# Attention and SwiGLU on one core: loads of batch 0 pair by pair, products from unit 5 on, and the rest tokens placed last in X

## The chip, the cores and the metric

The kernel runs on one core of one Trainium2 chip. The metric is the device time of one execution in microseconds (us), as a median of several. Before the change it is 454.04 us (three runs, 453.96 to 454.45). The profile is of one further execution, with a span of 453.1 us from the first to the last instruction.

## The reference, cut to what matters

Attention with 8 batches, 12 heads, 448 tokens and 64 values per head comes first; its output, as 3584 rows of 768, is the input of a SwiGLU block with 1536 inner columns.

```python
def _attn_ref(q, k, v):                      # (8, 12, 448, 64) each
    scale = 1.0 / np.sqrt(q.shape[-1])
    scores = scale * np.matmul(q, k.transpose(0, 1, 3, 2))
    scores = scores - np.max(scores, axis=-1, keepdims=True)
    attn = np.exp(scores)
    attn = attn / (np.sum(attn, axis=-1, keepdims=True) + 1e-09)
    return np.matmul(attn, v)

def _moe_ref(x, w_gate, w_val, w_out):       # x: (3584, 768)
    g = x @ w_gate                           # w_gate, w_val: (768, 1536)
    silu = g * (1.0 / (1.0 + np.exp(-g)))
    val = x @ w_val
    return silu * val @ w_out                # w_out: (1536, 768)
```

Inputs and output are float32. The kernel casts to fp16 while it loads.

## The kernel before

Two heads are one pair; there are 48 pairs, six per batch. The 448 keys of a pair are cut into four chunks of 112. The first 24 steps of the program are *units* (pair and chunk of batch 0); after them come *visits*, which mix chunks of later pairs with pieces of the SwiGLU block.

Loads of q, k, v and weights are requests of GpSimd (they cast). `load_qk16(pr, n)` fetches n pairs of q and k, `load_v(pr, n)` the values of n pairs, 112 KB a pair as fp16; `copy_v` moves the values beside a column of ones.

```python
        load_qk16(1, 1)
        make_identity(nc, ident)
        load_qk16(2, 1)
        load_qk16(3, 1)
        load_v(0, GP)              # GP = 3 pairs in one request
        load_qk16(4)               # two pairs
        load_v(3, GP)
        dummy(7)                   # filler matmuls
        prep(0)()
        dummy(1)
        turn = prep(1)
        wq = {                     # pair -> requests given out at its chunk 1
            0: [("qk", 6), ("g", 0), ("v", 0)],
            1: [("qk", 8), ("g", 1), ("v", 1)],
            3: [("qk", 10), ("V", 2), ("g", 2), ("v", 2)],
            4: [("g", 3), ("v", 3), ("qk", 12)],
            6: [("V", 3), ("o", 0)],
            7: [("o", 1)],
        }
```

In the program's list of waits each GpSimd request waits for the landing of the eighth request before it, as eight semaphores serve them in turn.

`prep(pr)` turns q and k of a pair, so that the 64 values lie on partitions: on TensorE for pairs 1 to 10, by DMA transposes (L168, L172) from pair 11 on. `qk` forms the scores of a chunk (L218) and takes their exponential on ScalarE (L226). `pv_chunk` multiplies it with values (L244, L252). The queries of a pair are cut into three blocks of 128 and a *rest* of 64, tokens 0 to 63; the two heads' rests share one block of 128 partitions. After the fourth chunk the sums are normalized into `xt`, and `turn_x` turns `xt` into X, the input of the SwiGLU block: channels on partitions, tokens along.

```python
        nc.vector.reciprocal(r[:, 0:7], a7[:, :, D])                      # L264
        nc.vector.tensor_tensor(xt..., a7[:, 0:n, 0:D], r..., ALU.mult)   # L265, n = 7 if pr < 12 else 6
        if pr < XPE:                                                      # XPE = 12
            return
        for hx in range(2):                                               # L274: the rest, pairs from 12 on
            nc.vector.tensor_scalar(xt[0:D, 3, ts(hx, D)], a7[ts(hx, D), 6, 0:D], r[ts(hx, D), 6:7], None, ALU.mult)
    # ... turn_x(pr) ...
        if pr < XPE:
            # tp is a PSUM tile
            for j in range(3):                                            # L292
                nc.tensor.matmul(tp[:, ds(D + 128 * j, 128)], lhsT=xt[:, j], rhs=ident[:], start=True, stop=True)
            for hx in range(2):                                           # L296: the rest
                nc.tensor.matmul(tp[ts(hx, D), 0:D], lhsT=xt[:, 3, 0:D], rhs=ident[:, ts(hx, D)], start=True, stop=True)
            nc.vector.tensor_copy(dst, tp[:, 0:S])                        # L303
            return
        nc.sync.dma_start_transpose(dst[:, D:S]..., xt[:, 0:3]...)        # L305
        nc.sync.dma_start_transpose(dst[:, 0:D]..., xt[0:D, 3])           # L308
```

The loop over units, with `dst` above being the pair's 448 tokens of X:

```python
        XAT = (11, 15, 17, 20)                       # units that begin with a turn_x
        for u in range(FIRST * NC):                  # 24 units
            pr, c = divmod(u, NC)
            qk(pr, c)
            # ... units 1 and 3: fillers and the turn of pair 1; unit 4: prep(2)()
            elif u >= 6 and c == 2:
                prep(pr + 2)()                       # pairs 3 to 7; pair 6 in unit 18
            if u in (5, 6, 7):
                dummy(1)
            if u in (6, 14):
                for p in range(3):
                    copy_v(u // 8 * 3 + p)
            if c == 1:
                for w in wq.pop(pr, []):
                    emit(w)
            if u in XAT:
                turn_x(XAT.index(u))
            for _ in range(1 if c == 2 or u in XAT else 2):
                if u >= 8 and pieces[0][0] * NC + pieces[0][1] <= u - 3:
                    piece()                          # one pv_chunk
```

The SwiGLU block works on blocks of 384 or 512 columns of X: block 0 on tokens 0 to 383 of batch 0, block 1 on the last 64 of batch 0 and all of batch 1, and so on. Each step makes a gate group `gp` and a value group `vp` of six matmuls (L317); the second part multiplies with `wo` (L362), evicts on ScalarE (L369) and writes rows of the output (L381).

Of the kernel before, what the change touches and what calls it, by code (L numbers as in the profile page):

```python
# [13 lines left out]
ALU = mybir.AluOpType  # L14
# [4 lines left out]
GP = 3  # L19
# [3 lines left out]
FIRST = 6  # L23
WIDE = 8
XPE = 12
# [8 lines left out]
def kernel(  # L34
# [14 lines left out]
    P = 112  # L49
# [6 lines left out]
    GPB = NHP // GP  # L56
    sm_scale = float(D) ** -0.5
    OH = DM // 2

    tabs = list(get_activation_tables(nc.m.arch).keys())  # L60

# [56 lines left out]
    def load_qk16(pr, n=2):  # L118
        h0 = 2 * (pr % 2) if pr >= 14 else 0
        if h0 == 0:  # L120
            q16 = raws.tile([P, 4, NC, D], FP16, tag="rq", bufs=RB, name="q16")
            k16 = raws.tile([P, 4, NC, D], FP16, tag="rk", bufs=RB, name="k16")
            pairbuf[:] = [q16, k16]
        q16, k16 = pairbuf
        for dst, src in ((q16, q), (k16, k)):
            flat = src.rearrange("b h s d -> (b h) s d")[2 * pr : 2 * pr + 2 * n]
            nc.gpsimd.dma_start(dst[:, ds(h0, 2 * n)], flat.rearrange("h (p c) d -> p h (c d)", c=NC))  # L127
        for i in range(n):
            h = h0 + 2 * i
            raw[pr + i] = (q16[:, h : h + 2], k16[:, h : h + 2])  # L130

    def load_v(pr, n=1):
        b, h = divmod(2 * pr, H)
        nc.gpsimd.dma_start(  # L134
            vraw[:, ds(pr % VS, n)].rearrange("p r h c d -> p (r h) (c d)"),
            v[b, h : h + 2 * n].rearrange("h (p c) d -> p h (c d)", c=NC),
        )

    def copy_v(pr):
        nc.vector.tensor_copy(Vts[pr % NV][:, :, :, 0:D], vraw[:, pr % VS])  # L140
# [91 lines left out]
                between()  # L232

    accs = {}

    def pv_chunk(pr, c):
        if c == 0:
            accs[pr] = ps_f.tile([128, 512], FP32, tag="f", name="acc")
        e = Es[pr % NE]
        vo = Vts[pr % NV]  # L240
        a7 = accs[pr][:, 0 : 7 * (D + 1)].rearrange("p (s d) -> p s d", s=7)
        for j in range(3):
            for hx in range(2):
                nc.tensor.matmul(  # L244
                    a7[:, 2 * j + hx],
                    lhsT=e[:, ds(c * EB + 9 * hx + 2 * j, 2)].rearrange("p b x -> p (b x)"),
                    rhs=vo[:, hx, c, 0 : D + 1],
                    start=c + j + hx == 0,
                    stop=False,
                )  # L250
        for hx in range(2):
            nc.tensor.matmul(  # L252
                a7[:, 6],
                lhsT=e[:, ds(c * EB + 6 + hx, 2)].rearrange("p b x -> p (b x)"),
                rhs=vo[:, hx, c, 0 : D + 1],
                start=False,
                stop=c == NC - 1 and hx == 1,
            )
        if c < NC - 1:
            return  # L260
        r = attp.tile([128, 8], FP32, tag="R", bufs=2, name="R")
        xt = Xts[pr % NX]
        n = 7 if pr < XPE else 6
        nc.vector.reciprocal(r[:, 0:7], a7[:, :, D])  # L264
        nc.vector.tensor_tensor(  # L265
            xt[:].rearrange("p j (h d) -> p (j h) d", h=2)[:, 0:n],
            a7[:, 0:n, 0:D],
            r[:, 0:n].unsqueeze(2).to_broadcast([128, n, D]),
            ALU.mult,
        )  # L270
        if pr < XPE:
            return
        for hx in range(2):
            nc.vector.tensor_scalar(  # L274
                xt[0:D, 3, ts(hx, D)], a7[ts(hx, D), 6, 0:D], r[ts(hx, D), 6:7], None, ALU.mult
            )

    def pv(pr):
        for c in range(NC):
# [2 lines left out]
    def turn_x(pr):  # L282
        b, hp = divmod(pr, NHP)
        kk, bb = divmod(b, NB)
        if kk not in X:
            X[kk] = xp.tile([128, NCB, NB * S], FP16, tag="X", name="X")
        dst = X[kk][:, hp, ts(bb, S)]
        xt = Xts[pr % NX]
        if pr < XPE:
            tp = accs[pr] if pr < FIRST else ps_f.tile([128, 512], FP32, tag="f", name="xtp")  # L290
            for j in range(3):
                nc.tensor.matmul(  # L292
                    tp[:, ds(D + 128 * j, 128)], lhsT=xt[:, j], rhs=ident[:], start=True, stop=True
                )
            for hx in range(2):
                nc.tensor.matmul(  # L296
                    tp[ts(hx, D), 0:D],
                    lhsT=xt[:, 3, 0:D],
                    rhs=ident[:, ts(hx, D)],
                    start=True,  # L300
                    stop=True,
                )
            nc.vector.tensor_copy(dst, tp[:, 0:S])  # L303
            return
        nc.sync.dma_start_transpose(  # L305
            dst[:, D:S].rearrange("p (j q) -> p j q", j=3), xt[:, 0:3].rearrange("p j m -> p (j m)")
        )
        nc.sync.dma_start_transpose(dst[:, 0:D].rearrange("p (j q) -> p j q", j=1), xt[0:D, 3])  # L308

    gate_small = [False]  # L310

# [32 lines left out]
    def ffn2_steps(kk, c0, n, hts, first, last_block):  # L344
        chunks = range(n // 128)
        if first:
            steps = [(ch, oh) for oh in range(2) for ch in chunks]
        else:
            steps = [(ch, oh) for ch in chunks for oh in range(2)]
        osbs = {}  # L350
        for ch, oh in steps:
            last = last_block and ch == n // 128 - 1
            if last or oh == 0:
                osbs[ch] = fp.tile([128, DM], FP32, tag="osb", bufs=3, name="osb")
            osb = osbs[ch]
            parts = [(oh * OH, OH)]
            if last and oh:
                parts = [(OH, OH // 2), (OH + OH // 2, OH // 2)]
            for m0, w in parts:
                op = ps_f.tile([128, 512], FP32, tag="f")  # L360
                for fb in range(NFB):
                    nc.tensor.matmul(  # L362
                        op[:, 0:w],
                        lhsT=hts[:, fb, ts(ch, 128)],
                        rhs=wo[oh][:, fb, ds(m0 - oh * OH, w)],
                        start=(fb == 0),
                        stop=(fb == NFB - 1),
                    )
                nc.scalar.activation(osb[:, ds(m0, w)], op[:, 0:w], AF.Copy, scale=1.0 / HS)  # L369
                if not last:  # L370
                    m0, w = 0, DM
                    if oh == 0:
                        continue
                l0 = c0 + ch * 128
                l = l0
                while l < l0 + 128:
                    b, j = divmod(l, S)
                    c, p0 = divmod(j, P)
                    m = min(P - p0, l0 + 128 - l)
                    eng = nc.scalar if last and m < 64 else nc.sync  # L380
                    eng.dma_start(  # L381
                        out[ts(NB * kk + b, S), :].rearrange("(p c) m -> c p m", c=NC)[
                            c, p0 : p0 + m, ds(m0, w)
                        ],
                        osb[l - l0 : l - l0 + m, ds(m0, w)],
                    )
                    l += m
            yield NFB * OH / 2400.0

# [6 lines left out]
    with tc.manual_schedule():  # L396
# [4 lines left out]
        for vo in Vts:  # L401
            nc.vector.memset(vo[:, :, :, D:], 1.0)
        load_qk16(1, 1)
        make_identity(nc, ident)
        load_qk16(2, 1)
        load_qk16(3, 1)
        load_v(0, GP)
        load_qk16(4)
        load_v(3, GP)
        dummy(7)  # L410
        prep(0)()
# [1 line left out]
        turn = prep(1)  # L413

        wq = {
            0: [("qk", 6), ("g", 0), ("v", 0)],
            1: [("qk", 8), ("g", 1), ("v", 1)],
            3: [("qk", 10), ("V", 2), ("g", 2), ("v", 2)],
            4: [("g", 3), ("v", 3), ("qk", 12)],
# [45 lines left out]
        def share(total, at, n):  # L465
            return (at + 1) * total // n - at * total // n

        XAT = (11, 15, 17, 20)
        pieces = [(p, c) for p in range(FIRST) for c in range(NC)]

        def piece():
# [2 lines left out]
        for u in range(FIRST * NC):  # L474
            pr, c = divmod(u, NC)
            qk(pr, c)
            if u == 1:
                dummy(1)
                turn()
                dummy(1)  # L480
            elif u == 3:
                dummy(2)
            elif u == 4:
                prep(2)()
            elif u >= 6 and c == 2:
                prep(pr + 2)()
            if u in (5, 6, 7):
                dummy(1)
            if u in (6, 14):
                for p in range(3):  # L490
                    copy_v(u // 8 * 3 + p)
            if c == 1:
                for w in wq.pop(pr, []):
                    emit(w)
            if u in XAT:
                turn_x(XAT.index(u))
            for _ in range(1 if c == 2 or u in XAT else 2):
                if u >= 8 and pieces[0][0] * NC + pieces[0][1] <= u - 3:
                    piece()

        queue = []
# [126 lines left out]
```

The softmax here doesn't subtract the row's maximum and nothing guards it: scores larger than these inputs give would overflow.

## Time and profile before

| engine or transfer | busy, us | share of 453.1 us |
|---|---|---|
| TensorE matmuls (PE) | 443.6 | 98% |
| TensorE weight loads (PEld, beside the matmuls) | 247.1 | 55% |
| VectorE (DVE) | 201.3 | 44% |
| ScalarE (ACT) | 239.1 | 53% |
| GpSimd (POOL) | 138.0 | 30% |
| GpSimd's DMA queue | 23.37 MB | 41.7% of 16 DMA engines |
| SyncE's DMA queue | 24.66 MB | 29.6% of 16 DMA engines |

"PE" counts a matmul from its start to its modelled end, and matmuls overlap, so its share says that the engine is occupied, not that it is at its peak. A wait is shown in brackets after an instruction: the time for which the engine stood idle before it, and what ended that. GpSimd's requests and SyncE's DMA instructions are shown with the time that it took to issue them; the landing is a number of its own ("DMA to landing").

### The profile page before, as it was taken

Reading aid. Unit: us, or ns where it says so; the run is one execution under the profiler, and the core shown is the slowest. Engines: PE = TensorE matmul, PEld = TensorE weight load, DVE = VectorE, ACT = ScalarE, POOL = GpSimd, SP = SyncE. Lnnn points to the kernel's source line nnn. Section 1 sums busy time; section 2 is a strip of 40 time slices with the busy share of each in tenths; the row PEclk is TensorE's granted clock in tenths of the full one; section 3 lists DMA queues with packets and bytes.
Section 4 is the critical chain, followed back from the end, with each engine's and each line's share of the span. In section 5 each row is a group of like instructions: output and inputs, shape, how many; then the busy total and the mean of one; then the engine's idle time right before and its main releaser. Section 6 shows DMA issues by size and latency. Waiting matters only on the chain.

```text
span 453.1 us, 9845 instructions
## 1 busy us (share of the span) xinstructions
PE 443.6 (98%) x4007; PEld 247.1 (55%) x4007; DVE 201.3 (44%) x456; ACT 239.1 (53%) x350; POOL 138.0 (30%) x222
## 2 busy tenths in 40 slices
PE   8889999999999999999999999999999999999996
PEld 3555655645455656545456665545455656644464
DVE  3555653356563535354443553444354444145400
ACT  6874576766555555645556446644654644222222
POOL 8454715927453225252322504440100000000000
PEclk9999999999999999999999999999999999999999
DMA  8999999999787739983867837974323102110033
GB/s 131 192 199 201 182 179 166 176 213 139 99 106 109 84 79 148 135 102 80 138 62 118 129 72 119 148 87 84 73 41 78 46 12 80 49 34 1 0 106 104
DMA packets 104941, 48.71 MB, mean 108 GB/s; under 512 B 59584, under 2 KB 101440, under 8 KB 104896
## 3 DMA queue, kind: packets, MB, share of 16 engines
q0 software_dynamic: 43296, 23.37, 41.7%
q1 hardware_dynamic: 61504, 24.66, 29.6%
q8 instruction: 31, 0.51, 0.4%
q14 instruction: 14, 0.11, 0.1%
q10 hardware_dynamic: 96, 0.05, 0.0%
HBM read 47.19 MB, written 11.01 MB: 128 GB/s over the span
## 4 chain that ended last, share of the span: by engine, by line
PE 90%; DMA 4%; DVE 2%; ACT 2%; POOL 1%; issue 1%; DVEq 0%; ACTq 0%; POOLq 0%
PE op L362 24%; PE gp L317 23%; PE vp L317 23%; PE acc L244 8%; PE s L218 8%; DMA vraw<-in_v_dram 4%; PE acc L252 2%; ACT E L226 1%; PE tp L206 1%; DVE t L336 1%; POOL k L127 0%; ACT sg L332 0%; DVE qkT L207 0%; POOL q L127 0%; DVE vo L140 0%
## 5 line engine op out<-in xcount | busy, mean ns | idle before, releaser
L226 ACT ACTIVATE E<-s 112x896 f16<-112x896 f32 x192 | 162.6, 918 | 29.9 <-PE s L218 29.3
L317 PE MATMUL vp<-X,wv 128*128 128x384 f16 (+1 forms) x576 | 124.7, 353 | 0.4 <-DVE qkT L210 0.4
L317 PE MATMUL gp<-X,wg 128*128 128x384 f16 (+1 forms) x576 | 124.7, 352 | 0.0
L362 PE MATMUL op<-wo,hts 128*128 128x384 f16 (+1 forms) x684 | 116.0, 323 | 0.0
L336 DVE SCALAR_TENSOR_TENSOR t<-sg,gp 128x384 f32<-128x384 f32 (+1 forms) x96 | 59.6, 621 | 120.7 <-ACT sg L332 120.7
L332 ACT ACTIVATE sg<-gp 128x384 f32<-128x384 f32 (+1 forms) x96 | 52.4, 546 | 85.2 <-PE gp L317 84.0
L362 PEld LDWEIGHTS <-hts 128*128 128x128 f16 x684 | 65.5, 98 | 45.9 <-issue 3.9
L317 PEld LDWEIGHTS <-wv 128*128 128x128 f16 x576 | 56.3, 98 | 53.3 <-DVE qkT L210 0.8
L317 PEld LDWEIGHTS <-wg 128*128 128x128 f16 x576 | 53.1, 97 | 45.6 <-issue 1.1
L369 ACT ACTIVATE osb<-op 128x384 f32<-128x384 f32 (+1 forms) x57 | 27.7, 487 | 92.5 <-PE op L362 91.0
L339 DVE SCALAR_TENSOR_TENSOR hts<-t,vp 128x384 f16<-128x384 f32 (+1 forms) x96 | 59.6, 621 | 10.8 <-PE vp L317 0.5
L165 POOL COPY qk<-q 112x512 f16<-112x512 f16 x37 | 22.9, 619 | 129.2 <-DMA qkT<-qk 128.0
L244 PEld LDWEIGHTS <-E 112*128 112x128 f16 x1152 | 46.3, 97 | 19.1 <-issue 16.6
L244 PE MATMUL acc<-vo,E 112*128 112x65 f16 x1152 | 53.0, 193 | 2.3 <-DVE vo L140 1.3
L218 PE MATMUL s<-qkT 64*128 64x448 f16 x384 | 50.4, 353 | 0.6 <-DVE qkT L195 0.3
L252 PE MATMUL acc<-vo,E 112*128 112x65 f16 x384 | 42.9, 193 | 0.0
L264 DVE RECIPROCAL R<-acc 128x7 f32<-128x7 f32 x48 | 9.8, 205 | 73.8 <-PE acc L252 73.8
L134 POOL DMA_DIRECT2D vraw<-in_v_dram x40 | 26.7, 667 | 31.2 <-DVE vo L140 17.9
L127 POOL DMA_DIRECT2D k<-in_k_dram x42 | 27.8, 662 | 10.3 <-DMA wo<-in_moe_w_out_dram 7.2
L127 POOL DMA_DIRECT2D q<-in_q_dram x42 | 28.0, 667 | 4.2 <-PE tp L206 1.7
L218 PEld LDWEIGHTS <-qkT 64*128 64x128 f16 x384 | 14.6, 94 | 26.4 <-issue 19.6
L265 DVE TENSOR_TENSOR xt<-acc,R 128x384 f16<-128x384 f32 (+1 forms) x48 | 27.6, 575 | 1.7
(42 smaller groups left out, 150.6 us busy)
## 6 DMA issues: line engine op xcount, KB each, us to landing
q<-in_q_dram POOLq DMA_DIRECT2D x37, 112.0 KB, 3.9
k<-in_k_dram POOLq DMA_DIRECT2D x37, 112.0 KB, 4.4
vraw<-in_v_dram POOLq DMA_DIRECT2D x36, 112.0 KB, 4.5
out_dram<-osb SPq DMA_DIRECT2D x7, 336.0 KB, 3.3
wg<-in_moe_w_gate_dram POOLq DMA_DIRECT2D x8, 288.0 KB, 11.5
wv<-in_moe_w_val_dram POOLq DMA_DIRECT2D x8, 288.0 KB, 11.2
wo<-in_moe_w_out_dram POOLq DMA_DIRECT2D x2, 1152.0 KB, 22.6
out_dram<-osb SPq DMA_DIRECT2D x8, 288.0 KB, 3.3
```

The costliest lines, as they stand in the source:

```text
L127: nc.gpsimd.dma_start(dst[:, ds(h0, 2 * n)], flat.rearrange("h (p c) d -> p h (c d)", c=NC))
L218: nc.tensor.matmul(s[:, hx, 0:S], lhsT=t[ts(hx, 64), c * P : c * P + 128], rhs=t[ts(hx, 64), ds(S + (1 - hx) * D, S)], start=True, stop=True,)
L226: nc.scalar.activation(e[:, :, 0:S], s[0:P, :, 0:S], AF.Exp, scale=sm_scale)
L244: nc.tensor.matmul(a7[:, 2 * j + hx], lhsT=e[:, ds(c * EB + 9 * hx + 2 * j, 2)].rearrange("p b x -> p (b x)"), rhs=vo[:, hx, c, 0 : D + 1] ...
L252: nc.tensor.matmul(a7[:, 6], lhsT=e[:, ds(c * EB + 6 + hx, 2)].rearrange("p b x -> p (b x)"), rhs=vo[:, hx, c, 0 : D + 1], start=False, st ...
L265: nc.vector.tensor_tensor(xt[:].rearrange("p j (h d) -> p (j h) d", h=2)[:, 0:n], a7[:, 0:n, 0:D], r[:, 0:n].unsqueeze(2).to_broadcast([12 ...
L317: nc.tensor.matmul(dst[:, 0:n], lhsT=wslice(kind, fb, cb), rhs=X[kk][:, cb, ds(c0, n)], start=(cb == 0), stop=(cb == NCB - 1),)
L332: nc.scalar.activation(sg[:, 0:n], gp[:, 0:n], AF.Tanh, scale=0.5)
L336: nc.vector.scalar_tensor_tensor(t1[:, 0:n], sg[:, 0:n], 1.0, gp[:, 0:n], ALU.add, ALU.mult)
L339: nc.vector.scalar_tensor_tensor(hts[:, fb, 0:n], t1[:, 0:n], 0.5 * HS, vp[:, 0:n], ALU.mult, ALU.mult)
L362: nc.tensor.matmul(op[:, 0:w], lhsT=hts[:, fb, ts(ch, 128)], rhs=wo[oh][:, fb, ds(m0 - oh * OH, w)], start=(fb == 0), stop=(fb == NFB - 1),)
L369: nc.scalar.activation(osb[:, ds(m0, w)], op[:, 0:w], AF.Copy, scale=1.0 / HS)
```

## The change

The change has five parts.

1. Requests. q and k of pairs 1 to 5 are fetched pair by pair, and the values of pairs 0, 1 and 2 each by its own request between them. q and k of pairs 6 and 7 are requested after the first quarter of gate and value weights, and no longer before it. This is to bring the first values in sooner.
2. Pieces of the product with the values begin in unit 5 and not 8; each `copy_v` has a unit of its own (`CAT`); the fillers of units 5 to 7 go.
3. The rest tokens (0 to 63 of each batch) are placed last in X, in columns 384 to 447 of a batch. Block 0 then reads no rest.
4. The rests of all pairs are turned by a DMA transpose (L309 of the changed kernel); for pairs below 12 this replaces the two matmuls of L296. Pairs below 12 normalize the rest by two VectorE operations of 64x64 (L275), as those from 12 on did before.
5. The output rows follow the new order of tokens: where a run of 128 rows is cut into writes moves, and so does their number.

```diff
+    MQ = S - D
@@ pv_chunk
-        n = 7 if pr < XPE else 6
         nc.vector.reciprocal(r[:, 0:7], a7[:, :, D])
-        nc.vector.tensor_tensor(... [:, 0:n], a7[:, 0:n, 0:D], ...)
-        if pr < XPE:
-            return
-        for hx in range(2):
-            nc.vector.tensor_scalar(xt[0:D, 3, ts(hx, D)], ...)
+        nc.vector.tensor_tensor(xt[:, 0:3]..., a7[:, 0:6, 0:D], ...)
+        def rest():
+            for hx in range(2):
+                nc.vector.tensor_scalar(xt[0:D, 3, ts(hx, D)], ...)
+        if pr == FIRST - 1:
+            rests[pr] = rest
+        else:
+            rest()
@@ turn_x
-                nc.tensor.matmul(tp[:, ds(D + 128 * j, 128)], lhsT=xt[:, j], rhs=ident[:], ...)
-            for hx in range(2):
-                nc.tensor.matmul(tp[ts(hx, D), 0:D], lhsT=xt[:, 3, 0:D], rhs=ident[:, ts(hx, D)], ...)
-            nc.vector.tensor_copy(dst, tp[:, 0:S])
-            return
-        nc.sync.dma_start_transpose(dst[:, D:S]..., xt[:, 0:3]...)
-        nc.sync.dma_start_transpose(dst[:, 0:D]..., xt[0:D, 3])
+                nc.tensor.matmul(tp[:, ts(j, 128)], lhsT=xt[:, j], rhs=ident[:], ...)
+            nc.vector.tensor_copy(dst[:, 0:MQ], tp[:, 0:MQ])
+            if pr in rests:
+                rests.pop(pr)()
+        else:
+            nc.sync.dma_start_transpose(dst[:, 0:MQ]..., xt[:, 0:3]...)
+        nc.sync.dma_start_transpose(dst[:, MQ:S]..., xt[0:D, 3])
@@ ffn2_steps, output rows
-                    c, p0 = divmod(j, P)
-                    m = min(P - p0, l0 + 128 - l)
+                    c, p0 = divmod((j + D) % S, P)
+                    m = min(P - p0, l0 + 128 - l, (MQ if j < MQ else S) - j)
                     eng = nc.scalar if last and m < 64 else nc.sync
@@ requests
         load_qk16(2, 1)
+        load_v(0)
         load_qk16(3, 1)
-        load_v(0, GP)
-        load_qk16(4)
+        load_v(1)
+        load_qk16(4, 1)
+        load_v(2)
+        load_qk16(5, 1)
         load_v(3, GP)
-            0: [("qk", 6), ("g", 0), ("v", 0)],
+            0: [("g", 0), ("v", 0), ("qk", 6)],
@@ units
-        XAT = (11, 15, 17, 20)
+        XAT = (11, 15, 17, 21)
+        CAT = (4, 7, 11, 14, 17, 21)
-            if u in (5, 6, 7):
-                dummy(1)
-            if u in (6, 14):
-                for p in range(3):
-                    copy_v(u // 8 * 3 + p)
+            if u in CAT:
+                copy_v(CAT.index(u))
-            for _ in range(1 if c == 2 or u in XAT else 2):
-                if u >= 8 and pieces[0][0] * NC + pieces[0][1] <= u - 3:
+            for _ in range(2 if c == 3 else int(c != 2 or u > 12)):
+                if u >= 5 and pieces[0][0] * NC + pieces[0][1] <= u - 3:
                     piece()
```

More of the change, by code (lines that the diff above doesn't have):

```diff
@@ L234 @@
     accs = {}
+    rests = {}
     def pv_chunk(pr, c):
@@ L262, in pv_chunk @@
         xt = Xts[pr % NX]
-        n = 7 if pr < XPE else 6
         nc.vector.reciprocal(r[:, 0:7], a7[:, :, D])
         nc.vector.tensor_tensor(
-            xt[:].rearrange("p j (h d) -> p (j h) d", h=2)[:, 0:n],
-            a7[:, 0:n, 0:D],
-            r[:, 0:n].unsqueeze(2).to_broadcast([128, n, D]),
+            xt[:, 0:3].rearrange("p j (h d) -> p (j h) d", h=2),
+            a7[:, 0:6, 0:D],
+            r[:, 0:6].unsqueeze(2).to_broadcast([128, 6, D]),
             ALU.mult,
         )
-        if pr < XPE:
-            return
-        for hx in range(2):
-            nc.vector.tensor_scalar(
-                xt[0:D, 3, ts(hx, D)], a7[ts(hx, D), 6, 0:D], r[ts(hx, D), 6:7], None, ALU.mult
-            )
+        def rest():
+            for hx in range(2):
+                nc.vector.tensor_scalar(
+                    xt[0:D, 3, ts(hx, D)], a7[ts(hx, D), 6, 0:D], r[ts(hx, D), 6:7], None, ALU.mult
+                )
+        if pr == FIRST - 1:
+            rests[pr] = rest
+        else:
+            rest()
     def pv(pr):
@@ L292, in turn_x @@
                 nc.tensor.matmul(
-                    tp[:, ds(D + 128 * j, 128)], lhsT=xt[:, j], rhs=ident[:], start=True, stop=True
+                    tp[:, ts(j, 128)], lhsT=xt[:, j], rhs=ident[:], start=True, stop=True
                 )
-            for hx in range(2):
[L296 to L302, printed above, removed]
-            nc.vector.tensor_copy(dst, tp[:, 0:S])
-            return
[L305 to L308, printed above, removed]
+            nc.vector.tensor_copy(dst[:, 0:MQ], tp[:, 0:MQ])
+            if pr in rests:
+                rests.pop(pr)()
+        else:
+            nc.sync.dma_start_transpose(
+                dst[:, 0:MQ].rearrange("p (j q) -> p j q", j=3),
+                xt[:, 0:3].rearrange("p j m -> p (j m)"),
+            )
+        nc.sync.dma_start_transpose(dst[:, MQ:S].rearrange("p (j q) -> p j q", j=1), xt[0:D, 3])
     gate_small = [False]
```

## The prediction

> **What bounds the kernel now.** I read the page first: TensorE (PE) is busy 443.6 of 453.1 us and carries 90% of the chain that ended last; the rest of that chain is mainly one transfer, the values (`vraw`), with 4%. So only two things can move the time: matmul work, and the few places where PE waits. The table of stages says where those are.
>
> ```profile
> core 0: us, PE busy (x) PEld busy (x) DVE busy (x) ACT busy (x) POOL busy (x), PEclk, DMA share, GB/s
> 0.00:8.00 8.00, 6.34 (x48) 2.59 (x49) 3.26 (x18) 4.56 (x8) 6.83 (x15) 1.00 0.80 129
> 8.00:15.00 7.00, 5.57 (x74) 2.81 (x74) 2.18 (x8) 5.88 (x8) 4.50 (x8) 1.00 1.23 156
> ...
> 30.00:40.00 10.00, 8.48 (x91) 4.88 (x88) 5.75 (x13) 5.22 (x8) 5.34 (x7) 1.00 1.37 200
> ...
> 100.00:150.00 50.00, 49.92 (x441) 26.21 (x438) 28.06 (x62) 29.56 (x42) 24.41 (x40) 1.00 0.94 115
> ```
>
> All idle PE time is in the first 60 us; from 100 us on nothing is to be had but less matmul work. In the same stages the transfers run at about 200 GB/s from 15 to 50 us, a flat level that I read as their limit. The PE timeline then names the waits of the start:
>
> ```profile
> 13.90 0.36 PE L244 MATMUL acc<-vo,E 112*128 112x65 f16 x6 [1.27 <-DVE vo L140]
> ...
> 24.29 0.39 PE L206 MATMUL tp<-ident,q 112*64 112x112 f16 x8
> ...
> 32.63 0.34 PE L292 MATMUL acc<-ident,xt 128*128 128x128 f16 x3 [0.96 <-DVE xt L265]
> ...
> 33.05 1.15 PE L317 MATMUL gp<-X,wg 128*128 128x384 f16 x6
> ```
>
> The first product of batch 0 waits 1.27 us for values; the first FFN group starts at 33.05. (The line at 24.29 is the turning of pair 6, which we need below.) The chain shows what comes after:
>
> ```profile
> 27.73 10.92 DMA vraw<-in_v_dram
> 38.67 0.30 DVE vo L140
> 38.97 0.53 DVE qkT L207
> 39.50 0.11 DVE qkT L210
> 39.61 0.04 issue
> 39.65 1.15 PE vp L317 x6
> ```
>
> The values of pairs 6 to 8 land at 38.67. VectorE works in order: their copy, then the eviction of pair 8's turned q and k, and only then does the PSUM buffer come free in which PE writes `vp` at 39.65. PE waits 0.44 us there. This is a gate: however early the start ends, PE is not past it before the landing plus 1.0 us.
>
> **What the Trainium skill says.** "DMA: Bandwidth & Descriptors", section "Issuing engines are not separate DMA queues": requests of SyncE, ScalarE and GpSimd run on the same 16 DMA engines and interleave. The trace agrees: between 53 and 70 us, while the first DMA transposes run, the GpSimd queue falls from about 200 to about 145 GB/s. Same page, "Rules for kernel authors": a transfer under 64 KB is mostly overhead. One rest transpose moves 64x128 fp16, 16 KB. In a quiet stage it lands 2.3 us after its issue; the same shape for q and k in the full stage takes four times that:
>
> ```profile
> DMA to landing us min/median/max: 9.7/10.3/11.0
> ```
>
> "Perfetto Trace Analysis", "DMA Instruction — SWDGE (GPSIMD)": the profiled end of such an instruction is the end of writing descriptors, not of moving data. So here: a GpSimd request is busy 0.65 to 0.78 us, but lands 4 to 11 us after its issue; only landings are used below.
>
> **The change part by part.** *Matmuls removed.* Twelve pairs lose two rest matmuls (L296) each. On the timeline the pair of them takes 0.15 us of PE's sequence (17.18 to 17.33), so 12 x 0.15 = 1.8 us, of which six pairs (0.9 us) lie before the gate and cannot count, and six (0.9 us) lie between 40 and 82 us, where PE is full. Three filler matmuls of 0.3 us in units 5 to 7 also lie before the gate.
>
> *Values earlier.* Before, the values of pair 0 came in one request of three pairs, issued at 5.86 and landed at 13.5. Now 112 KB of them stand behind q and k of pair 2; I expect about 9 us, counting the bytes ahead of them. That takes away the 1.27 us wait, and with products from unit 5 the exponentials (0.85 us each, ScalarE) would set the pace of the start: unit 18 is reached at about 6.3 + 17 x 0.86, say 21 us, instead of 24.
>
> *q and k of pairs 6 and 7 later.* They now stand behind the first gate and value weights (4 x 288 KB). Before, they were issued at 8.79 and landed 10.2 and 10.6 us later, at 19.0 and 20.1; the last of the four weights landed at 14.98 + 10.9 = 25.9. The bytes up to the last of these requests are the same in both kernels and the queue is full, so k of pair 6 now lands at about 25.9. Pair 6 is turned on PE in unit 18. PE would be there at 21 and waits until 26: 4 to 5 us. From there on, units 19 to 23 need five exponentials (4.3 us), then the last product piece, its normalization, the turn and the eviction (about 2.2 us as between 30.8 and 33.0 before). First FFN group: 26.7 + 0.6 + 4.3 + 2.2, about 34, one later than before. So the early values are, by my sum, given back.
>
> *The gate.* The bytes ahead of the values of pairs 6 to 8 are the same, too. To them come about four rest transposes; one is 64 packets of 256 B, and in the stage 53 to 70 packets of the two queues alternate one for one, so each takes the place of 64 weight packets of 768 B, 49 KB, or 0.25 us. That is +1.0. The later first FFN group asks for the same size: gate +1.0, say 40.7 for 39.65.
>
> *Rest of pair 11.* Block 1 reads X of all of batch 0 and half of batch 1's tokens, rests included. It now needs a DMA that the matmuls did not. Its place on SyncE's queue is that of the L305 line here:
>
> ```profile
> 82.59 1.23 SPq L172 DMA_TRANSPOSE qkT<-qk  x1
> 83.93 1.01 SPq L381 DMA_DIRECT2D out_dram<-osb  x2
> 85.04 1.25 SPq L305 DMA_TRANSPOSE X<-xt  x1
> ```
>
> Those ahead of it wait for GpSimd's casts, which run without a gap from 73.4, when the second half of `wo` has landed. Landing takes 5 to 7.6 us in this stage, so 90.5 to 92.5. The matmul that needs it is the sixth of the group that began at 89.42, at 90.5. With gate and removed matmuls PE comes at 90.5 + 1.0 - 0.9 = 90.6; SyncE is itself later by one to two (eight rest transposes at 0.25 delay `wo`). Wait 1 to 2 us, estimate 1.5.
>
> *Later.* Pairs from 12 on had both DMA transposes before; nothing changes but the order of tokens. *End.* The last 128 rows were 112 by SyncE beside 16 by ScalarE; now they are 64 and 64, both on SyncE, one issue (0.4 to 0.5 us) after the other: +0.45.
>
> Sum: gate +1.0, matmuls -0.9, rest of pair 11 +1.5, end +0.45: +2.05, 456.1. I take 455.6, as the two waits are estimated from transfers whose latency I know only to a microsecond or two.
>
> **The rivals.** (a) *The start's gain goes through.* If the early transfers are faster in the new order (129 GB/s in the first 8 us, 156 in the next 7, against 200 later, so there is room of up to 1.5 us), the gate opens earlier, and the rest of pair 11 lands in time: -1.5 - 0.9 + 0.45, about 452. For it: the change removes real work and the room is there. Against: the gate lies on bytes, which are not fewer. (b) *A longer wait.* With a pause of 4 to 5 us and three fillers less, PE could lose its granted clock for some microseconds, or the transposes disturb the full stage more than by their packets: in the timeline of transfers the whole stream nearly stops for 0.8 us at 55.3 and again at 66.4, both with transposes in flight and never before 52 us. Six such pauses before 40 us would make 459. For it: the two dips. Against: one transpose is small. (c) *Everything hidden.* Gate and rest of pair 11 both as before, end +0.45, matmuls -0.9: 453.6.
>
> **Range and chances.** My sum lies between (c) and (b). Range 452.6 to 459.0. A change of 2% is 9.1 us: none of the rivals reaches it. Faster by over 2%: 0.01; within: 0.97; slower: 0.02.
>
> **What would show it right or wrong.** Right: first product near 10.9 us instead of 13.9; PE waiting 3 to 5 us ahead of pair 6's turn, released by the DMA of q or k; first FFN group at 33.5 to 34.5; `vp` of the second visit behind `vo L140` at 40 to 41.5; PE waiting 1 to 2 us near 90 us for an X transpose of L309; PE from 100 us on as before. Wrong: q of pair 6 landing before 22 us, which would bring the first FFN group under 31; values of pairs 6 to 8 landing before 38; or a wait near 90 us that is missing.

## The result, and the profile after

The changed kernel takes 459.79 us as a median of four runs (458.38 to 460.22); the kernel before took 454.25 us in the same session (453.96 to 454.71). The ratio is 1.0116, with a 95% interval of 1.009 to 1.0141: it is slower by about 5.5 us. The profiled execution has a span of 457.6 us, 4.5 more than before, and the rest of this section says where these 4.5 us are.

I start at the same places as the prediction. This is the PE timeline of the changed kernel (start in us, duration, instruction, count, and in brackets the idle time before it and what ended that):

```profile
11.37 0.34 PE L246 MATMUL acc<-vo,E 112*128 112x65 f16 x6 [0.79 <-DVE vo L141]
...
25.77 0.39 PE L207 MATMUL tp<-ident,q 112*64 112x112 f16 x8 [3.05 <-DMA q<-in_q_dram]
26.84 0.58 PE L207 MATMUL tp<-ident,k 112*64 112x112 f16 x8 [0.68 <-DMA k<-in_k_dram]
...
37.36 1.14 PE L318 MATMUL gp<-X,wg 128*128 128x384 f16 x6
...
92.88 1.46 PE L318 MATMUL gp<-X,wg 128*128 128x512 f16 x6
```

The first product begins 2.5 us earlier than before, but the first FFN group begins 4.31 us later (37.36 for 33.05), and block 1 3.46 us later (92.88 for 89.42). The waits for q and k end at 26.84, and yet 10.52 us pass from there to the first FFN group. In the kernel before, the same stretch, from the turn of pair 6's k to the first FFN group at 33.05, takes 8.54 us; the second line here is its block 1:

```profile
24.51 0.36 PE L206 MATMUL tp<-ident,k 112*64 112x112 f16 x8
...
89.42 1.46 PE L317 MATMUL gp<-X,wg 128*128 128x512 f16 x6
```

So the 4.31 us are two things: pair 6's k is turned 2.33 us later (26.84 for 24.51), and the stretch behind it is 1.98 us longer. The chain of the changed kernel shows the cause of the waits (start, duration, what):

```profile
14.91 11.89 DMA k<-in_k_dram
26.79 0.04 issue
26.84 0.58 PE tp L207 x4
```

k of pairs 6 and 7 lands at 26.79, behind the four weight requests. What comes after the wait is in the table of stages of the same kernel. Its seventh number, ahead of the DMA share, is the granted clock:

```profile
core 0: us, PE busy (x) PEld busy (x) DVE busy (x) ACT busy (x) POOL busy (x), PEclk, DMA share, GB/s
26.00:27.00 1.00, 0.32 (x12) 0.17 (x8) 0.00 (x0) 0.00 (x0) 0.70 (x1) 0.80 1.42 194
27.00:28.00 1.00, 1.00 (x18) 0.77 (x16) 0.53 (x1) 0.00 (x0) 0.68 (x2) 0.50 1.39 199
...
32.00:33.00 1.00, 1.00 (x18) 0.73 (x16) 0.01 (x1) 0.55 (x1) 0.71 (x1) 0.50 1.35 199
33.00:34.00 1.00, 1.00 (x19) 0.60 (x16) 0.73 (x3) 0.37 (x1) 0.61 (x1) 0.79 1.41 195
```

A mean of 0.80 in the slice from 26 us is 0.6 us at full and 0.4 us at half clock; 0.79 in the slice from 33 us is the reverse. So PE worked at half clock from 26.6 to 33.4, through units 18 to 22, and from 26.84 on it was busy all of that time.

The end is the third place. The last eviction starts at 453.05, so 4.55 us before the end; before, it started at 449.59, 3.51 us before the end:

```profile
453.05 0.33 ACT L370 ACTIVATE osb<-op 128x192 f32<-128x192 f32 x1 [0.61 <-PE op L363]
```

```profile
449.59 0.33 ACT L369 ACTIVATE osb<-op 128x192 f32<-128x192 f32 x1 [0.56 <-PE op L362]
```

One line of the source view (count: least, median and longest issue in ns, first and last start) of the kernel after, and one of the kernel before, show why:

```profile
L382 SPq DMA_DIRECT2D out_dram<-osb x6: 472/568/596, 451.6 to 454.7; - x6
```

```profile
L381 SPq DMA_DIRECT2D out_dram<-osb x3: 316/317/317, 448.2 to 449.9; - x3
```

Both count the writes of the last 128 rows. Before, three more went out on ScalarE's queue beside these. Now all are on SyncE, each takes 0.57 us in place of 0.32, and the last is issued 1.65 us after the last eviction started, not 0.3.

The ledger of the two traces: first FFN group +4.31; from there to block 1 -0.85 (55.52 for 56.37); from block 1 to the output's last run of matmuls 0.00 (338.49 in both); end +1.04. The sum is +4.50, which is the difference of the spans.

### The profile page after: what moved, and what is told of

Read it like the earlier page. It is cut to its first block, busy times and chain, and to the rows that moved or that the text cites. A ratio compares the mean times of both kernels' runs of the same rounds, so it can differ in the third digit from the quotient of the medians. Undisturbed runs are those within 1.5% of the kernel's fastest.

```text
span 457.6 us, 9845 instructions
## 1 busy us (share of the span) xinstructions
PE 444.0 (97%) x3980; PEld 247.8 (54%) x3980; DVE 206.4 (45%) x480; ACT 238.9 (52%) x350; POOL 140.3 (31%) x226
## 4 chain that ended last, share of the span: by engine, by line
PE 89%; DMA 5%; DVE 2%; ACT 2%; POOL 1%; issue 1%; POOLq 0%; DVEq 0%; ACTq 0%
PE op L363 24%; PE gp L318 23%; PE vp L318 23%; PE acc L246 8%; PE s L219 8%; DMA k<-in_k_dram 4%; PE acc L254 2%; ACT E L227 1%; DMA vraw<-in_v_dram 1%; PE tp L207 1%; DVE t L337 1%; ACT sg L333 1%; POOL q L128 0%; POOL k L128 0%; DVE xt L266 0%
## 5 line engine op out<-in xcount | busy, mean ns | idle before, releaser
L246 PEld LDWEIGHTS <-E 112*128 112x128 f16 x1152 | 47.5, 98 | 19.0 <-issue 18.2
L246 PE MATMUL acc<-vo,E 112*128 112x65 f16 x1152 | 53.9, 195 | 1.6 <-DVE vo L141 0.8
L254 PE MATMUL acc<-vo,E 112*128 112x65 f16 x384 | 43.3, 194 | 0.0
L135 POOL DMA_DIRECT2D vraw<-in_v_dram x42 | 27.9, 664 | 26.4 <-DVE vo L141 12.7
L266 DVE TENSOR_TENSOR xt<-acc,R 128x384 f16<-128x384 f32 x48 | 26.7, 557 | 1.7
```

The costliest lines, as they stand in the source:

```text
L135: nc.gpsimd.dma_start(vraw[:, ds(pr % VS, n)].rearrange("p r h c d -> p (r h) (c d)"), v[b, h : h + 2 * n].rearrange("h (p c) d -> p h (c ...
L246: nc.tensor.matmul(a7[:, 2 * j + hx], lhsT=e[:, ds(c * EB + 9 * hx + 2 * j, 2)].rearrange("p b x -> p (b x)"), rhs=vo[:, hx, c, 0 : D + 1] ...
L254: nc.tensor.matmul(a7[:, 6], lhsT=e[:, ds(c * EB + 6 + hx, 2)].rearrange("p b x -> p (b x)"), rhs=vo[:, hx, c, 0 : D + 1], start=False, st ...
```

## The experiments

My theory (A) from these traces was that q and k of pair 6, late behind the weights, cost the time: by the wait itself and by the clock that it takes away. The rivals were that the rest transposes on SyncE's queue cost it, by the traffic or by what waits for them, and that the gate (the values of pairs 6 to 8) would hold PE anyway. Times below are medians of each kernel; those of the kernel before, beside them on the same chip, are between 454.41 and 454.59. Ratios are to these, with a 95% interval.

**1. q and k of pair 6 first again.**

```diff
-            0: [("g", 0), ("v", 0), ("qk", 6)],
+            0: [("qk", 6), ("g", 0), ("v", 0)],
```

> The changed kernel with one line undone: q and k of pairs 6 and 7 are requested ahead of the first gate and value weights again. Theory A (the wait for q and k of pair 6, 3.05 + 0.68 us, and the seven us of halved TensorE clock behind it are the loss): no wait in unit 18, clock 1.00 from 20 to 40 us, first FFN group at 30 to 32, then a wait for the values of pairs 6 to 8 with vp of the second visit at about 40; 454.0 to 455.0 us in all. Rival B (the loss comes from the rest transposes, the longer VectorE work and the new order of units): first FFN group still after 35, 458 us or more.

Measured: 459.04 us (457.75 to 462.96), ratio 1.0111 [1.0062, 1.0159]. PE timeline of the profiled execution, which was the slowest (462.96), then its stages:

```profile
30.46 1.14 PE L318 MATMUL gp<-X,wg 128*128 128x384 f16 x6
...
39.83 1.15 PE L318 MATMUL vp<-X,wv 128*128 128x384 f16 x6 [2.81 <-DVE qkT L211]
...
94.87 0.58 PE L318 MATMUL gp<-X,wg 128*128 128x512 f16 x1 [4.46 <-DMA X<-xt]
```

```profile
95.00:97.00 2.00, 2.00 (x6) 0.63 (x5) 0.69 (x1) 0.60 (x1) 0.83 (x2) 0.50 1.15 184
...
100.00:101.00 1.00, 1.00 (x6) 0.40 (x5) 0.00 (x0) 0.46 (x1) 0.00 (x0) 0.85 1.35 223
```

The start is won: the first FFN group comes at 30.46, 6.9 us before that of the changed kernel. It is then lost twice. PE stands at the gate for 2.81 us, and near 90 us for 4.46 us, because the rest of pair 11 is still on its way: its DMA transpose (L309) is issued at 89.35 and lands 5.5 us later. The clock falls to half within this second wait and stays there until 100.3. In the changed kernel both transfers are there as well: the values land at 38.7, and the rest of pair 11, issued at 86.94, lands at 92.2. PE comes so late that it waits for neither. In 1 the transpose is issued 2.4 us later than that, behind four transposes of q and k on SyncE's queue; why these are later was not followed up. Theory A names the right first cause, and not all of the cost.

**2. Fillers in the wait.** Twelve filler matmuls of 0.23 us ahead of pair 6's turn keep PE busy while it waits.

```diff
+                if pr == 4:
+                    wp = ps_s.tile([128, 2, 512], FP32, tag="s", name="wp")
+                    for _ in range(12):
+                        nc.tensor.matmul(wp[:, 0], lhsT=warm[:, 0:128], rhs=warm[:], ...)
                 prep(pr + 2)()
```

> The changed kernel with 12 filler matmuls (0.22 us each, 2.6 us) in unit 18 ahead of the turning of pair 6, where TensorE stands idle for 3.05 us. If the halved clock after the idle stretch is a part of the loss of its own: clock stays at 1.00, the first FFN group comes at about 34 and not 37.4, 456 to 457 us in all. If only the late landing counts: no change, 459.8. If the fillers cost what they take: 462.

Measured: 461.13 us (458.59 to 462.93), ratio 1.0138 [1.0096, 1.018]. PE timeline, stages and, under them, one line of the list of waits (total, times, longest):

```profile
27.05 0.39 PE L207 MATMUL tp<-ident,k 112*64 112x112 f16 x8 [1.01 <-DMA k<-in_k_dram]
...
35.31 1.14 PE L318 MATMUL gp<-X,wg 128*128 128x384 f16 x6
```

```profile
20.00:30.00 10.00, 7.90 (x103) 4.53 (x99) 4.65 (x14) 4.88 (x7) 5.19 (x8) 1.00 1.41 194
30.00:40.00 10.00, 8.32 (x109) 5.08 (x106) 6.51 (x17) 5.20 (x7) 5.11 (x8) 1.00 1.45 185
```

```profile
PE gp L318 <- DMA X<-xt: 3.4, 1, 3.4
```

The clock stays at full from 20 to 40 us, and the first FFN group comes at 35.31, 2.05 us earlier. From the turn of pair 6's k to there are 8.26 us, for 10.52 in the changed kernel: these 2.26 us are the clock's part in this pair of executions. The whole is no faster, as PE now comes early enough to wait 3.4 us for the rest of pair 11. Here, too, a gain at the start was spent at the next obstacle.

**3. The kernel before, with only the order of this one request changed.**

```diff
-            0: [("qk", 6), ("g", 0), ("v", 0)],
+            0: [("g", 0), ("v", 0), ("qk", 6)],
```

> The kernel before with one line of the change: q and k of pairs 6 and 7 requested behind the first gate and value weights. Theory A: TensorE, which comes to unit 18 at 24.3 there, waits until about 26.8, 2.5 us; if the clock falls after so short a wait too, about 458, if it does not, 455.5 to 456.5. Rival B: within 0.5 us of 454.3.

Measured: 458.63 us, ratio 1.0076 [1.0026, 1.0126], with a wide spread: 454.99 us in the execution that kept a clock of 1.000, 457.47 at 0.993, 459.78 at 0.985 and 460.28 at 0.984. The profile is of the last of these. PE timeline, then stages:

```profile
24.28 0.39 PE L206 MATMUL tp<-ident,q 112*64 112x112 f16 x8 [0.26 <-DMA q<-in_q_dram]
25.40 0.39 PE L206 MATMUL tp<-ident,k 112*64 112x112 f16 x8 [0.73 <-DMA k<-in_k_dram]
...
37.12 2.10 PE L317 MATMUL gp<-X,wg 128*128 128x384 f16 x6
```

```profile
25.00:30.00 5.00, 4.29 (x53) 2.51 (x53) 2.08 (x5) 2.57 (x4) 3.33 (x5) 0.74 1.36 201
30.00:35.00 5.00, 5.00 (x63) 3.23 (x62) 2.08 (x5) 3.68 (x5) 2.50 (x4) 0.50 1.38 198
35.00:40.00 5.00, 4.04 (x25) 2.11 (x23) 1.67 (x4) 0.49 (x1) 2.60 (x4) 0.50 1.36 201
40.00:45.00 5.00, 5.00 (x42) 2.67 (x41) 2.92 (x7) 1.96 (x3) 2.35 (x4) 0.89 1.31 202
```

The two waits add up to 1 us, and the first FFN group still comes 4.1 us later than in the kernel before; its six matmuls take 2.10 us, not 1.15. Of the 4.1 us, 0.9 are the later turn of pair 6's k (25.40 for 24.51), and 3.2 are the stretch behind it at half clock (11.72 us for 8.54). In the one execution that kept the clock the same line costs 0.6 us (454.99 against 454.41), which is within the spread of the kernel before. So of all five parts of the change this one line is enough for most of the loss, and most of what it costs is clock.

**4. Rests of pairs 0 to 11 by matmul again** (in the changed kernel, its request order kept).

```diff
+            for hx in range(2):
+                nc.tensor.matmul(tp[ts(hx, D), MQ:S], lhsT=xt[:, 3, 0:D], rhs=ident[:, ts(hx, D)], ...)
-            nc.vector.tensor_copy(dst[:, 0:MQ], tp[:, 0:MQ])
+            nc.vector.tensor_copy(dst, tp[:, 0:S])
+            return
```

> The changed kernel with the rests of pairs 0 to 11 turned by two matmuls again and normalized in one VectorE operation (rest tokens stay last in X, requests and pieces stay as changed). Theory A: start as late as in the changed kernel, and 12 x 0.15 us of matmuls come back, six of them behind the wait in unit 18 or later: 460 to 461. Rival B (rest transposes by DMA and two 64x64 operations of VectorE a pair hold up the start): 456 to 458.

Measured: 460.18 us (458.08 to 462.98), ratio 1.0116 [1.0062, 1.017]. The waits for q and k remain (1.9 and 0.7 us) and the first FFN group is at 37.91. Taking the transposes of the rests away alone gives nothing: they don't make the start late, and near 90 us PE comes too late to need them early.

**5. Both: edits 1 and 4.**

> The changed kernel with q and k of pairs 6 and 7 first again and the rests of pairs 0 to 11 turned by matmuls. Theory A2 (three waits stand one behind the other, and each long one halves the clock after it: q and k of pair 6; values of pairs 6 to 8; rest of pair 11): the first and the third are gone, the second stays, so first FFN group at about 30.5, vp of the second visit at about 39.8 after a wait of 2.5 to 3 us, block 1 at 89.5 without a wait, clock 1.00 from 90 us on, and the time is that of the kernel before plus the longer end (1.04 us): 455.0 to 456.0. If the rest transposes had nothing to do with the wait near 90 us: 458 to 460 as without them.

Measured: 455.46 us (455.39 to 455.61), ratio 1.0013 [0.9984, 1.0043]; the clock is between 0.997 and 1.000 in all four. PE timeline:

```profile
38.90 1.15 PE L332 MATMUL vp<-X,wv 128*128 128x384 f16 x6 [1.90 <-DVE qkT L211]
...
88.66 1.46 PE L332 MATMUL gp<-X,wg 128*128 128x512 f16 x6
```

Each edit alone left the time at 459 to 460; together they take 4.3 us away. The only wait of size that is left is the gate, and block 1 runs through.

**6. Edit 1, and only pair 11's rest by matmul.**

```diff
+            if pr == XPE - 1:
+                # the two matmuls of edit 4, into tp[:, MQ:S]
+                nc.vector.tensor_copy(dst, tp[:, 0:S])
+                return
```

> As the run before, but only the rest of pair 11 is turned by matmuls; pairs 0 to 10 keep their rest transposes. Theory A2: the last rest to land is the one that block 1 waits for, so the wait near 90 us goes with this one pair, unless the rest of pair 10 lands after 90 us too. Five pairs times 0.15 us of matmuls are saved behind the gate: 454.5 to 455.3, and 0.5 us below the run before. Rival: the wait near 90 us only moves to another rest, 457 or more.

Measured: 457.34 us (456.05 to 459.71), ratio 1.006 [1.0015, 1.0105]. No wait is left near 90 us, but the gate is later. PE timeline:

```profile
40.61 1.15 PE L332 MATMUL vp<-X,wv 128*128 128x384 f16 x6 [3.58 <-DVE qkT L211]
```

The values of pairs 6 to 8 land at 39.6 and not at 37.9 as in 5; the kernels differ in the rests of pairs 0 to 10, of which those of batch 0 are transposed in this stage. That they delay the full stage is not shown: the same values land at 38.8 in 7, whose rests are those of 6, at 38.8 in 1 and 38.7 in the changed kernel, where all rests are transposed by DMA, and at 38.7 in the kernel before, where none of these is.

**7. Edit 6, and the second half of the last rows on ScalarE's queue.**

```diff
-                    eng = nc.scalar if last and m < 64 else nc.sync
+                    eng = nc.scalar if last and j >= MQ else nc.sync
```

> As the run before, and of the last 128 rows the second 64 are written from ScalarE's queue and not from SyncE's. From the start of the last eviction to the end the changed kernel takes 4.55 us and the kernel before 3.51. Theory: the two writes one after the other on SyncE cost this; the stretch comes back to about 3.5 and the time falls by 1.0. Rival: it is the size of the writes (64 rows of 768 B and not 16 and 112), the stretch stays at 4.5.

Measured: 456.63 us (455.97 to 458.67), ratio 1.0046 [1.0008, 1.0084]. From the last eviction to the end are 3.53 us, against 4.63 in 6 and 3.51 in the kernel before: the whole of the end's loss comes back. Its medians differ from 6 by 0.7 us, which the spread of either covers; the end is read from the trace.

**8. Edit 7, and the values of pairs 6 to 8 requested ahead of q and k of pair 10.**

```diff
-            3: [("qk", 10), ("V", 2), ("g", 2), ("v", 2)],
+            3: [("V", 2), ("qk", 10), ("g", 2), ("v", 2)],
```

> As the run before, and the values of pairs 6 to 8 are requested ahead of q and k of pairs 10 and 11 (2 x 224 KB, 2.2 us of the full queue). Theory A2: the gate in the second visit opens about 2.2 us earlier, vp at about 37.6 and not 39.8, and as nothing waits behind it the whole time falls by 1.5 to 2.2 us: 452 to 452.7, below both kernels. Rival: q and k of pairs 10 and 11 now come too late or another transfer takes the place of the gate; no gain.

Measured: 453.93 us (452.7 to 455.0), ratio 0.9987 [0.995, 1.0024]. The wait at the gate falls from 2.3 to 0.16 us, and `vp` starts at 37.76. In 7 the wait was followed by half clock from 39.8 to 43.2; here the clock stays at full, so that the 2.7 us between the medians are more than the wait alone.

**9. All of it: edits 1, 4, 7 and 8.**

> The changed kernel with four parts mended: q and k of pairs 6 and 7 requested first, rests of pairs 0 to 11 by matmuls, second 64 of the last rows from ScalarE's queue, values of pairs 6 to 8 requested ahead of q and k of pairs 10 and 11. Theory A2: first FFN group at about 31, vp of the second visit at 37.5 to 37.8 with no or a short wait, no wait near 90 us, clock 1.00 behind the start, end 3.5 us after the last eviction begins: 455.46 - 1.0 (end) - 1.2 (gate) = 453.2 us, that is 0.9 to 1.5 us below the kernel before. Rival: another transfer takes the place of the gate, 454.5 or more.

Measured: 453.20 us (six runs, 452.36 to 454.89) against 454.41, ratio 0.9973 [0.9951, 0.9995]. This is 1.2 us below the kernel before, 0.3%, and the interval just leaves out 1. PE timeline:

```profile
30.82 1.15 PE L332 MATMUL gp<-X,wg 128*128 128x384 f16 x6
...
36.81 1.14 PE L332 MATMUL vp<-X,wv 128*128 128x384 f16 x6
...
86.56 1.46 PE L332 MATMUL gp<-X,wg 128*128 128x512 f16 x6
```

There is no bracket on any of the three lines. The first FFN group is 2.2 us earlier than in the kernel before, and block 1 2.9 us earlier.

**10. Edit 4 with the fillers of 2**: the request order of the change, no rest of pair 11 to wait for, and only the fillers as the difference from 4.

> The changed kernel with the rests of pairs 0 to 11 by matmuls (460.18 us, its clock between 0.981 and 0.996) and 12 filler matmuls ahead of the turning of pair 6. The wait for q and k of pair 6 stays, and no wait can take the gain near 90 us. If the halved clock behind a wait is a cost of its own: clock 0.999 to 1.00 in all runs, first FFN group at 35 to 36 and not 37.9, 456.5 to 458, with less spread from run to run. If the clock costs nothing by itself: 460 as without fillers.

Measured: 456.99 us (five runs: 456.41, 456.66, 456.99, 457.26, 461.17), ratio 1.005 [1.0024, 1.0077]. That is 3.2 us less than 4 (four of the five runs lie below all four of 4), for 2.8 us of matmuls whose result nobody reads. The profile is of the slowest of them, so no trace shows the gain itself, but its PE timeline shows a case in which the fillers were too short:

```profile
22.30 2.76 PE L501 MATMUL wp<-warm 128*128 128x512 f16 x12
26.59 0.39 PE L207 MATMUL tp<-ident,q 112*64 112x112 f16 x8 [1.52 <-DMA q<-in_q_dram]
27.80 0.39 PE L207 MATMUL tp<-ident,k 112*64 112x112 f16 x8 [0.82 <-DMA k<-in_k_dram]
```

Here q came later than the fillers lasted; PE waited 2.3 us after all, its clock was 0.50 from 30 to 35 us, and the run is 4.2 us over the median of the five.

**11. The kernel before with edit 8 alone.**

> The kernel before with one line of the best version: values of pairs 6 to 8 requested ahead of q and k of pairs 10 and 11. It asks whether the best version gains by this line alone, or by the change's earlier start that this line lets through. Theory A2: the gate opens two us earlier, but TensorE only waits 0.44 us there, so vp of the second visit comes at 39.2 and the gain is 0.4 us at most: 453.9 to 454.4, and 0.5 to 1 us above the best version. Rival: the line alone brings 1.2 us, 453.2.

Measured: 454.16 us (six runs, 453.37 to 454.81), ratio 0.9991 [0.9975, 1.0008]. `vp` starts at 38.39 without a wait, but the kernel before was at this gate for 0.44 us only. By the medians this line brings 0.3 us and 9 brings 1.2, though their intervals overlap. The larger part of the gain of 9 is then the earlier start of the change, let through the opened gate.

## Why the prediction was wrong

It said 455.6 us (452.6 to 459.0); measured were 459.79. By its own steps:

- *Values earlier.* Right: about 9 us for the landing of pair 0's values, measured 9.0 (issued at 4.57, 4.41 to landing); the first product at 10.9, measured 11.37, with 0.79 us of wait left.
- *q and k of pairs 6 and 7 later.* Right in mechanism. Landing at 25.9, measured 26.79 for k; a wait of 4 to 5 us, measured 3.05 + 0.68. The sum that follows starts from 26.7, which is close to the measured turn at 26.84 though the landing was 0.9 us off.
- *First FFN group: 26.7 + 0.6 + 4.3 + 2.2, about 34.* This is the step that failed. The terms from pair 6's turn on came to 7.1 us and took 10.52 (26.84 to 37.36). Of the 3.4 us that are missing, some 2.3 are the clock: PE was at half clock for 6.8 us, and in 2, where it stayed at full, the same stretch takes 8.26 us. That is less than half of the 6.8 us: PE's busy time in the stretch is 2.57 us longer than in 2 (9.21 for 6.64), and its idle time 0.31 us shorter. The other 1.2 us were missing at full clock too: the sum of single terms was too short for a stretch that takes 8.54 us in the kernel before, where the two lines of the prediction's own timeline, 24.29 and 33.05, lie 8.76 apart. Rival (b) named the clock, but its 459 was six pauses in the stream of transfers. No such pause is in the trace (a mean of 196 GB/s from 20 to 40 us), so that it lies near the measured time is luck. The Trainium skill, "TensorE: Matmul & The Clock Gate", section "Why this matters for your kernels", advises no idle gaps above about 3 us between matmuls; the predicted wait was over that, so the clock belonged in the sum as a term of its own. The trace of the changed kernel agrees (0.50 after 3.7 us of waits), those of 3 and 6 do not: in 3 the clock fell after 1 us of waits and some tenths beside them, and in 6 it stayed at full after 3.58 us at the gate (in 7 it fell after 2.32). The length of the gap alone does not decide it here.
- *The gate* (+1.0) and *rest of pair 11* (+1.5). As obstacles both exist: edit 1 meets them with 2.81 and 4.46 us. As terms of the sum they were wrong, and neither cost anything. The gate did not move: the values land at 38.7, as before (38.65), so the delay by rest transposes isn't there. The rest of pair 11 landed at 92.2, as predicted (90.5 to 92.5), but PE came 3.46 us late to block 1. Such waits don't add up; a transfer that has landed when PE gets there is free.
- *Matmuls removed* (-0.9). From the first FFN group to block 1 the change takes 0.85 us less. Of this 0.44 is the gate's wait that is gone, and a new wait of 0.25 for the rest's normalization goes against it, so that some 0.66 are left for the matmuls.
- *End* (+0.45). The mechanism was right and the size was not: +1.04. The issues on the one queue grew from 0.32 to 0.57 us each, and two late ones follow each other. Experiment 7 gives the whole back.
- *From 100 us on as before.* Right: 338.49 us from block 1 to the last run of matmuls, in both.

What stays open is why the clock falls after short waits in some executions and not in others; in 3 one execution of four kept it. The same page, section "What's actually happening", describes an activity window of about 3.4 us that runs freely, so that it is chance where a wait falls in it. The spread from run to run fits that, and so do the lengths of the half clock (below), but no run here shows where a window begins. Nor did I part the traffic of the rests from chance in 6.

## What to carry to other kernels

A wait of TensorE costs its own length and then, if the clock falls, a part of the microseconds behind it (2.3 us in the changed kernel, 3.2 in 3); a sum over a timeline at full clock has to carry that as a term. Fillers or an earlier request can take it away (3.2 us between the medians of 4 and 10). Where a stretch as a whole stands in a trace, take its length from there and not from a sum of its parts. Obstacles in a row don't add: before taking one away, write down when each later transfer lands and when the engine would now reach it, as this change won only when the late request, the rest of pair 11, the gate and the end were all dealt with. In the full stage the weights, q and k here landed in the order in which they were asked (the last weights at 24.9, q at 25.8, k at 26.8), so what is needed first should be asked first, and bytes for later may stand behind it.

## What the runs showed of the hardware that was not expected

- The half clock lasts longer than the wait that brought it: 6.8 us in the changed kernel, 13.7 us in 3 (0.74, 0.50, 0.50 and 0.89 in the slices of 5 us from 25 on make 2.6 + 5 + 5 + 1.1), although PE was busy 4 to 5 of every 5 us there, with small matmuls above all. Added up in this way, the half clock behind a wait has only three lengths in all traces: 3.4 us (in 2 near 95 us, and in 7), 6.8 (in the changed kernel, 1 and 10) and 13.7 (in 3 and 4), so one length once, twice and four times.
- 2.76 us of matmuls whose result nobody reads made a kernel 3.2 us faster by its median (10 against 4).
- A write of the output takes SyncE 0.57 us to issue at the end of the changed kernel and 0.32 at the end of the kernel before. The two differ in where rows are cut into writes and in the queues. In 7, with the cut of the changed kernel and two queues as before, it is 0.47, so the larger part of the growth stays with the cut.
- A DMA transpose of 16 KB lands 5.5 us after its issue at 89.35 in 1; in the same trace, at 102 us, it takes 2.3 us.
